# Cross-covariance attention into a gated feed-forward on one core: output weights on another queue, moved norm roots, a plain first chunk

## The chip, the cores and the metric

The kernel runs on one core of one Trainium2 chip. The core has four compute engines with instruction streams of their own: TensorE (PE, matrix products into the accumulator memory PSUM), VectorE (DVE), ScalarE (ACT) and GpSimd (POOL). A fifth, SyncE (SP), only issues transfers here. DMA transfers are issued from SP, ACT and POOL, and all move data through the same 16 DMA engines. An engine executes its instructions in program order, so an instruction that waits holds up everything behind it on that engine.

The metric is device time in microseconds: the median of several executions. A difference below about 0.5% is no difference.

## The reference, cut to what matters

```python
B, N, C = 4, 6016, 256                       # q, k, v: float32, times 0.1
qn = q / (norm(q, axis=1) + 1e-6)            # norms run over the 6016 rows
kn = k / (norm(k, axis=1) + 1e-6)
s  = kn^T @ qn / tau                         # 256 x 256 for each batch
a  = softmax(s)                              # over the last axis
x  = (v @ a).reshape(24064, 256)
gate = sigmoid(x @ w_gate)                   # 256 -> 1536
out  = (gate * (x @ w_val)) @ w_out          # 1536 -> 256
```

## The kernel before

A batch is handled in two parts. The first makes its attention matrix. For each of its 47 row tiles (128 rows each) `score` multiplies q against k into one PSUM tile (`ps_s`, two products of 128x256), and the squares of q and k are summed for the norms. For batch 0 this is the head of the program, and it runs at the pace at which q and k are loaded. For batches 1 to 3 it runs beside the feed-forward of the batch before. The softmax is then folded into the weights: `gh` multiplies the exponentials by `w_gate` and `w_val` and scales by the row sums (`rrow`, and half of it, `rhalf`). This gives G and H, so that v goes straight into the feed-forward.

The second part is the feed-forward. It runs over 12 chunks of a batch, four row tiles (512 rows) each and three in the last one, and in a chunk over 12 **slots**, one for each 128 of the 1536 hidden columns. So a batch has slots 0 to 143, and slot 120 is the first slot of chunk 10. In a slot `glu` does two products with G into `ps_gate`, two with H into `ps_val`, a tanh on ACT (`g_sb`), and one DVE instruction that makes a row of `hT` from `g_sb` and `ps_val`. `ps_gate` and `ps_val` have two buffers each.

The output product of a chunk runs one chunk later, seven matmuls of 128x128 in each slot (`run_work`). It doesn't multiply plainly. Two row tiles (a pair p) and two column halves are combined as in Strassen's scheme: seven products in place of eight, over sums of `hT` blocks (`a_sum`, DVE, tile `sums`, five for each half of the hidden columns) and sums of weight blocks (`sum_w_out`, POOL, tile `w_sums`). `part` copies three partial products out on ACT (`m_sb`) and adds them on POOL; `whole` copies the four results (`out_sb`) and corrects them on POOL. A chunk with four row tiles has two pairs; their order is in `ORDER`. The last chunk of a batch has three tiles: one lone pair and a single tile, whose 12 products of 128x256 (`single`) stand ahead of the pair's. The last chunk of all is finished behind the loop by `end_rows` and `last_rows`.

The order is written out by hand. Each engine's instructions stand in the order in which the Python code emits them, and `side_work` hangs extra calls on slots with `at(slot, function)`. What it hangs there for the next batch n:

- `load_qk`, `load_v` on POOL's queue; `score`, `acc_square`, `acc_add` up to slot 96; `acc_fold` at slots 97 to 117
- `norms_mm` at 119 (sums the squares over rows on PE), `root_seed` at 120 (two DVE instructions: first guess for the inverse root), `root_steps` at 120 (POOL: four Newton steps of four instructions and one product)
- `norms_inv` at 123 (two DVE instructions that read the root `r`), `spread_both` at 124 (PE: four passes that spread `r` over the partitions), `copy_rk` at 125, `scale_x` at 126 and 127, `exps` at 128 and 129, `sums_both` at 131, `gh` from 132 on

For batch 0, `load_w_out` at slots 0, 1 and 2 loads the output weights (three pieces of 512 KB, float32). The call stands at a slot, but it is on SP, which has nothing else to do, so only the piece's buffer holds it back. `copy_w_out` casts a piece on POOL and `sum_w_out` makes the sums of weights, 15 instructions. All other weights and nearly all q, k and v come over POOL's queue, which casts from float32 to bfloat16 on the way; its order is q and k of batch 0, v chunk 0, six weight pieces, v chunk 1.

In the head, `busy(n)` issues n products on constants that only keep PE busy.

Of the kernel before, what the change touches and what calls it, by code (L numbers as in the profile page):

```python
# [53 lines left out]
def kernel(  # L54
# [138 lines left out]
    def load_w_out(n):  # L193
        w_f32[n] = f32pool.tile([P, TPC, C], FP32, tag="f32", name="w_f32")
        nc.sync.dma_start(
            out=w_f32[n], in_=moe_w_out.rearrange("(t p) c -> p t c", p=P)[:, n * TPC : (n + 1) * TPC, :]
        )
# [156 lines left out]
    def root_steps(b):  # L354

        s = st[b]
        x, y = s["sq_n"], s["y"]
        t = attp.tile([P, 2 * CB], FP32, tag="tn", name="t_n")
        s["r"] = attp.tile([P, 2 * CB], FP32, tag="r", name="r")
        for _ in range(4):  # L360
            nc.gpsimd.tensor_tensor(out=t, in0=x, in1=y, op=ALU.mult)  # L361
# [3 lines left out]
        nc.gpsimd.tensor_tensor(out=s["r"], in0=x, in1=y, op=ALU.mult)  # L365
# [51 lines left out]
    def sums_both(b):  # L417
# [13 lines left out]
        invert(r, ps_r, 1e-9, 1.0)  # L431
        half = attp.tile([P, CB], FP32, tag="rhalf", name="rhalf", bufs=2)
        nc.vector.tensor_scalar(out=half, in0=r, scalar1=0.5, scalar2=None, op0=ALU.mult)
        s["rrow"] = [[x[:, i : i + 1] for i in range(CB)] for x in (r, half)]
# [119 lines left out]
    def out_work(b, ci):  # L554
# [5 lines left out]
        states = [{} for _ in range(half)]  # L560

# [49 lines left out]
        def single(s, f):  # L611
            if f == 0:
                states[0]["single"] = pso.tile([P, CH], FP32, tag="o", name="ps_o")
            ps = states[0]["single"]
# [63 lines left out]
    adds, ends = [], []  # L678
    for g, (t0, nt) in enumerate(groups0):
# [17 lines left out]
        if g == last0:  # L697
            norm_mms(ps_n0, acc, TPC, True, False)
            for n, (end, rows_n) in enumerate(ends):
                norm_mms(ps_n0, end, rows_n, False, n == len(ends) - 1, (1, 0) if n else (0, 1))  # L700
        for u in range(nt):
            score(0, t0, u)
        if n_acc - 4 <= g < n_acc:
            busy(1)
    st[0]["n"] = ps_n0
    norms_sqrt(0)
    nc.scalar.preload_act_table(ACT.Exp)
    norms_inv(0)
    copy_s(0, 0)
    copy_s(0, 1)  # L710
    busy(3)
# [14 lines left out]
    gh_store(0, 0, ps_first, False)  # L726
    gh(0, 1, psg, "g", act=True)
# [3 lines left out]
    def side_work(b):  # L731
# [7 lines left out]
        for ci in range(NCH):  # L739
# [34 lines left out]
        for i in range(6):  # L774
            at(8 * FC + 1 + 4 * i, acc_fold, n, *divmod(i, 3))
# [6 lines left out]
        at(s0 + 7, copy_rk, n)  # L782
        at(s0 + 8, scale_x, n, 0)
        at(s0 + 9, scale_x, n, 1)
        at(s0 + 10, exps, n, 0)
        at(s0 + 11, exps, n, 1)
        at(s0 + 13, sums_both, n)
        at(s0 + 13, gh_tiles, n)
        for i in range(len(gh_order)):
            at(s0 + 14 + i, gh, n, i, *((pss, "s"), (psm, "m"))[i % 2])  # L790
# [7 lines left out]
    for b in range(B):  # L798
        side = side_work(b)
        for ci in range(NCH):  # L800
            final = (b, ci) == (B - 1, NCH - 1)
            for f in range(FC):
                first = (b, ci, f) == (0, 0, 0)
                glu(b, ci, f, (lambda: gh(0, 4, pso, "o", act=False)) if first else None)
                if prev is not None:
                    if f == 4:
                        store()
                    if f in NEXT_SLOTS:
                        a_sum(*prev, 1, NEXT_SLOTS[f])
                    run_work(work, 1 / max(1, FC - 2 * final - f))  # L810
                if f in OWN_SLOTS and not final:
# [48 lines left out]
```

## Time and profile before

| | |
|---|---|
| median of 9 executions | 828.92 us (827.39 to 836.74) |
| the profiled execution | 831.71 us, of which its span is 829.9 us |
| granted TensorE clock, mean | 0.984 |
| PE / DVE / ACT / POOL busy | 96% / 87% / 63% / 43% |
| DMA moved | 78.24 MB, mean 94 GB/s |
| chain that ended last | PE 89%, DMA 4%, POOL 3%, DVE 2% |

The span runs from the first instruction to the last; 1.8 us of the execution lie around it. Rows of the timeline give start, duration, engine, line, operation, tile written and tile read, shapes and count, and in brackets the idle time of the engine before the row and what ended it. Every product has line L127, since one helper issues them all, so tiles are what tells them apart. A matmul's duration includes its way through the array; products that follow each other start closer together than that, so the distance between starts is the cost. Rows of the view by windows give the stretch, its length, the busy time of PE, weight loads (PEld), DVE, ACT and POOL with their counts, the granted clock, the share of the DMA engines and GB/s. Bytes are counted as written, so a load that casts from float32 counts half of what it reads.

### The profile page before, as it was taken

To read this page: it belongs to the slowest core of one execution; us is meant where nothing else is said; L and a number is where in the kernel's file an instruction comes from. 1 tells how busy PE (TensorE), PEld (TensorE's weight loads), DVE (VectorE), ACT (ScalarE), POOL (GpSimd) and SP (SyncE) were. 2 spreads that over 40 slices of the span, in tenths; PEclk is the share of its full clock that TensorE was granted. 3 is DMA by queue.
4 is the path that set the end of the run, shared out by engine and by line. 5 is a ranking of instruction groups with operands and counts; after the bars stand their busy time and mean duration, and the time that the engine had idled before them with its cause. 6 is when DMAs were issued, how large, how long until landed. Compare 5 with 4: busy or idle time off the path is not lost.

```text
span 829.9 us, 17993 instructions
## 1 busy us (share of the span) xinstructions
PE 793.2 (96%) x6790; PEld 503.9 (61%) x6790; DVE 725.3 (87%) x1240; ACT 526.8 (63%) x887; POOL 358.7 (43%) x583
## 2 busy tenths in 40 slices
PE   3699999999899999999899999999989999999997
PEld 2446666666566666666566666666656566666665
DVE  4788999999688999999887999999978899898994
ACT  3557777765466777775566777776656565666663
POOL 3455445434443444434543454433353234434442
PEclk9799999999899999999999999999999999999999
DMA  9984767532557756422446566623422332433301
GB/s 228 218 156 89 118 101 133 102 64 46 86 117 112 114 102 133 92 52 67 92 82 112 96 127 109 116 52 88 60 52 52 84 64 52 90 64 78 70 27 71
DMA packets 77929, 78.24 MB, mean 94 GB/s; under 512 B 50705, under 2 KB 55825, under 8 KB 77841
## 3 DMA queue, kind: packets, MB, share of 16 engines
q0 software_dynamic: 21216, 38.02, 28.3%
q1 hardware_dynamic: 56336, 38.48, 20.6%
q8 instruction: 53, 0.87, 0.4%
q10 hardware_dynamic: 288, 0.59, 0.2%
q14 instruction: 36, 0.29, 0.1%
HBM read 78.64 MB, written 24.64 MB: 124 GB/s over the span
## 4 chain that ended last, share of the span: by engine, by line
PE 89%; DMA 4%; POOL 3%; DVE 2%; issue 1%; ACT 1%; POOLq 0%
PE ps_gate L127 28%; PE ps_val L127 28%; PE ps_o L127 26%; PE ps_s L127 4%; DMA k_sb<-in_k_dram 4%; PE ps_gh L127 2%; DVE hT L517 1%; ACT g_sb L516 1%; PE ps_rk L127 0%; POOL t_n L363 0%; POOL t_n L362 0%; DVE sums L539 0%; POOL t_n L361 0%; POOL y_n L364 0%; POOL out_sb L607 0%
## 5 line engine op out<-in xcount | busy, mean ns | idle before, releaser
L516 ACT ACTIVATE g_sb<-ps_gate 128x512 f32<-128x512 f32 (+1 forms) x576 | 338.3, 588 | 244.0 <-PE ps_gate L127 232.5
L517 DVE SCALAR_TENSOR_TENSOR hT<-g_sb,ps_val 128x512 bf16<-128x512 f32 (+1 forms) x576 | 384.1, 670 | 72.4 <-ACT g_sb L516 57.2
L127 PE MATMUL ps_val<-vT,gh_H 128*128 128x512 bf16 (+1 forms) x1152 | 339.4, 376 | 0.9 <-DVE hT L517 0.8
L127 PE MATMUL ps_gate<-vT,gh_G 128*128 128x512 bf16 (+1 forms) x1152 | 339.5, 376 | 0.0
L539 DVE TENSOR_TENSOR sums<-hT 128x768 bf16<-128x768 bf16 (+1 forms) x470 | 288.3, 613 | 0.0
L127 PEld LDWEIGHTS <-sums 128*128 128x128 bf16 x2730 | 188.5, 98 | 89.9 <-issue 4.4
L127 PEld LDWEIGHTS <-gh_H 128*128 128x128 bf16 x1152 | 113.1, 98 | 133.7 <-issue 4.3
L606 POOL TENSOR_TENSOR out_sb<-out_sb,m_sb 128x256 f32<-128x256 f32 x91 | 78.4, 862 | 236.3 <-ACT out_sb L598 224.1
L127 PE MATMUL ps_o<-w_sums,sums 128*128 128x128 bf16 x1638 | 158.9, 219 | 1.7 <-DVE sums L539 1.7
L592 POOL TENSOR_TENSOR m_sb<-m_sb 128x128 f32<-128x128 f32 x91 | 42.7, 469 | 183.0 <-ACT m_sb L591 183.0
L127 PEld LDWEIGHTS <-hT 128*128 128x128 bf16 x1176 | 85.3, 98 | 44.5
L127 PEld LDWEIGHTS <-gh_G 128*128 128x128 bf16 x1152 | 97.3, 98 | 15.2 <-DVE gh_G L466 0.4
L127 PE MATMUL ps_o<-w_out_sb,sums 128*128 128x128 bf16 x1092 | 99.6, 221 | 2.0 <-ACT m_sb L591 1.9
L127 PE MATMUL ps_o<-w_sums,hT 128*128 128x128 bf16 x1092 | 97.7, 219 | 0.0
L127 PE MATMUL ps_s<-k_sb,q_sb 128*128 128x256 bf16 x376 | 71.9, 295 | 19.1 <-DMA k_sb<-in_k_dram 12.1
L607 POOL TENSOR_TENSOR out_sb<-out_sb 128x256 f32<-128x256 f32 x91 | 80.0, 879 | 7.1
L598 ACT COPY out_sb<-ps_o 128x512 f32<-128x512 f32 x91 | 53.4, 586 | 14.0 <-PE ps_o L127 11.2
L278 DVE TENSOR_TENSOR acc<-acc,sq 128x1024 bf16<-128x1024 bf16 (+1 forms) x66 | 60.4, 915 | 0.0
L593 POOL TENSOR_TENSOR m_sb<-m_sb 128x128 f32<-128x128 f32 x91 | 55.4, 608 | 7.1
L240 ACT ACTIVATE sq<-k_sb 128x1024 bf16<-128x1024 bf16 (+2 forms) x44 | 44.8, 1028 | 16.7 <-DMA k_sb<-in_k_dram 16.7
L127 PEld LDWEIGHTS <-q_sb 128*128 128x128 bf16 x376 | 33.7, 105 | 25.0 <-issue 12.6
L591 ACT COPY m_sb<-ps_o 128x384 f32<-128x384 f32 x91 | 43.6, 479 | 4.3 <-PE ps_o L127 2.0
(81 smaller groups left out, 309.1 us busy)
## 6 DMA issues: line engine op xcount, KB each, us to landing
out_dram<-out_sb SPq DMA_DIRECT2D x44, 512.0 KB, 3.4
v_sb<-in_v_dram POOLq DMA_DIRECT2D x44, 256.0 KB, 5.2
q_sb<-in_q_dram POOLq DMA_DIRECT2D x35, 256.0 KB, 4.3
k_sb<-in_k_dram POOLq DMA_DIRECT2D x35, 256.0 KB, 5.2
q_sb<-in_q_dram POOLq DMA_DIRECT2D x4, 512.0 KB, 14.0
k_sb<-in_k_dram POOLq DMA_DIRECT2D x4, 512.0 KB, 16.3
w_f<-in_moe_w_out_dram SPq DMA_DIRECT2D x3, 512.0 KB, 18.4
out_dram<-out_sb SPq DMA_DIRECT2D x3, 384.0 KB, 2.8
```

Of the source, the lines that this page charges most:

```text
L127: nc.tensor.matmul(out, lhsT=lhsT, rhs=rhs, start=start, stop=stop, **kw)
L240: nc.scalar.activation(out=sq[:, :nt, :], in_=src[:, :nt, :], func=ACT.Square)
L278: nc.vector.tensor_tensor(out=acc[:, :nt, :], in0=acc[:, :nt, :], in1=st[b]["sq", w][:, :nt, :], op=ALU.add)
L516: nc.scalar.activation(out=g_sb[:, :n], in_=ps_gate[:, :n], func=ACT.Tanh, scale=0.5)
L517: nc.vector.scalar_tensor_tensor(out=hts[b, ci][:, f, :n], in0=g_sb[:, :n], scalar=1.0, in1=ps_val[:, :n], op0=ALU.add, op1=ALU.mult,)
L539: nc.vector.tensor_tensor(out=sums[b, ci, g][:, m, :, : half * P], in0=hT[:, f0 + k0 : f1 : 2, ds(r0 * half * P, half * P)], in1=hT[:, f0 ...
L591: nc.scalar.copy(m, states[p]["ps"][:, : 3 * P].rearrange("p (n c) -> p n c", c=P))
L592: nc.gpsimd.tensor_tensor(out=m[:, 1, :], in0=m[:, 1, :], in1=m[:, 2, :], op=ALU.add)
L593: nc.gpsimd.tensor_tensor(out=m[:, 2, :], in0=m[:, 1, :], in1=m[:, 0, :], op=ALU.add)
L598: nc.scalar.copy(o[:, p : p + half + 1 : half, :], states[p]["ps"].rearrange("p (t c) -> p t c", c=C),)
L606: nc.gpsimd.tensor_tensor(out=ends, in0=ends, in1=states[p]["m"][:, 1:3, :], op=ALU.add)
L607: nc.gpsimd.tensor_tensor(out=ends, in0=ends, in1=mids, op=ALU.subtract)
```

## The change

Seven edits:

1. The three `w_out` loads are issued on POOL's queue, behind the other weights and v chunk 1, in place of SP. Their casts are at slot 8 and the sums of weights at slots 10 to 18.
2. For the next batch: three Newton steps in place of four; `norms_mm` at slot 117, `root_seed` and `root_steps` at 118, `norms_inv` at 124, `spread_both` at 125, `copy_rk` at 126, both `scale_x` at 127; the rest stays on its slots. `acc_fold` is closer together (97 to 115).
3. The single tile of a three-tile chunk stands between the lone pair's `z1` and `x2`, no longer ahead of the pair.
4. In the last chunk of all, the work is shared over all 12 slots (before: 10), and each `a_sum` of the second half stands one slot earlier.
5. Chunk 0 of batch 0 makes its output plainly: 48 products of 128x256, no `a_sum`, no `part`, no `whole`.
6. In the head: the last scores stand ahead of the last norm products; scores are copied out of PSUM ahead of the root, one half on ACT; q's norm is multiplied in by two DVE instructions (`scale_q`), and k's by one instruction for each block; `rhalf` is made after the first store of G.
7. `busy` gets other counts and places: 4, 1, 4, 4, 2 behind groups 6 to 10 (before: 1 each behind 7 to 10), then 2 (before 3).

```diff
-    def load_w_out(n):
+    for n in range(FC // TPC):
         w_f32[n] = f32pool.tile([P, TPC, C], FP32, tag="f32", name="w_f32")
-        nc.sync.dma_start(
+        nc.gpsimd.dma_start(
...
-        for _ in range(4):
+        for _ in range(3):
...
-        nc.vector.tensor_copy(out=s["x"][:, j, :], in_=s["s"][:, j, :])
+        (nc.scalar.copy if j else nc.vector.tensor_copy)(out=s["x"][:, j, :], in_=s["s"][:, j, :])
+
+    def scale_q(b, j):
+        s = st[b]
+        x = s["x"][:, j, :]
+        nc.vector.tensor_scalar(out=x, in0=x, scalar1=s["r"][:, j : j + 1], scalar2=None, op0=ALU.mult)
...
-        for j in range(CB):
-            nc.vector.scalar_tensor_tensor(
-                out=y[:, j, :],
-                in0=s["x"][:, j, ds(i * P, P)],
-                scalar=s["r"][:, j : j + 1],
-                in1=s["rk"][i],
-                op0=ALU.mult,
-                op1=ALU.mult,
-            )
+        nc.vector.tensor_tensor(
+            out=y,
+            in0=s["x"][:, :, ds(i * P, P)],
+            in1=s["rk"][i].rearrange("p (o c) -> p o c", o=1).to_broadcast([P, CB, P]),
+            op=ALU.mult,
+        )
...
+        plain = (b, ci) == (0, 0)
...
-        if nt % 2:
-            for f in range(FC):
-                work.append((2, single, nt - 1, f))
+        if plain:
+            return [(2, single, t, f) for t in range(nt) for f in range(FC)]
         for p, name in ORDER:
             if p < half:
                 for i in range(FC // 2):
                     work.append((1, product, p, name, i))
+                if nt % 2 and name == "z1":
+                    for f in range(FC):
+                        work.append((2, single, nt - 1, f))
...
-        if n_acc - 4 <= g < n_acc:
-            busy(1)
+        busy(fill.get(g, 0))
...
-                    at(i, load_w_out, i)
-                    at(i + 2, copy_w_out, i)
+                    at(8, copy_w_out, i)
                 for n, m in enumerate((1, 0, 3, 2, 4)):
                     for i in range(FC // TPC):
-                        at(3 + 3 * n + i, sum_w_out, m, i)
+                        at(10 + 2 * n, sum_w_out, m, i)
...
-        s0 = 10 * FC - 2
-        at(s0 + 1, norms_mm, n)
-        at(s0 + 2, root_seed, n)
-        at(s0 + 2, root_steps, n)
-        at(s0 + 5, norms_inv, n)
-        at(s0 + 6, spread_both, n)
+        s0 = 10 * FC - 3
+        at(s0, norms_mm, n)
+        at(s0 + 1, root_seed, n)
+        at(s0 + 1, root_steps, n)
+        at(s0 + 7, norms_inv, n)
+        at(s0 + 8, spread_both, n)
...
-                    if f in NEXT_SLOTS:
-                        a_sum(*prev, 1, NEXT_SLOTS[f])
-                    run_work(work, 1 / max(1, FC - 2 * final - f))
-                if f in OWN_SLOTS and not final:
+                    if f + final in NEXT_SLOTS and prev != (0, 0):
+                        a_sum(*prev, 1, NEXT_SLOTS[f + final])
+                    run_work(work, 1 / (FC - f))
+                if f in OWN_SLOTS and not final and (b, ci) != (0, 0):
```

How this stands on the engines, at two places. The first is POOL at the start of the program, behind the weights. `v_sb` is a chunk of v, `w_f32` a piece of the output weights, `q_sb` and `k_sb` are the first rows of batch 1. Before:

```order
L184 DMA w_val2_175<-in_moe_w_val_dram 128x2x512
L147 DMA v_sb_183<-in_v_dram 128x1024
L147 DMA v_sb_476<-in_v_dram 128x1024
L200 CAST w_out_sb_176<-w_f32_478 128x1024
L137 DMA q_sb_511<-in_q_dram 128x1024
L137 DMA k_sb_513<-in_k_dram 128x1024
L200 CAST w_out_sb_176<-w_f32_493 128x1024
```

Now:

```order
L184 DMA w_val2_175<-in_moe_w_val_dram 128x2x512
L147 DMA v_sb_183<-in_v_dram 128x1024
L195 DMA w_f32_186<-in_moe_w_out_dram 128x4x256
L195 DMA w_f32_188<-in_moe_w_out_dram 128x4x256
L195 DMA w_f32_190<-in_moe_w_out_dram 128x4x256
L147 DMA v_sb_501<-in_v_dram 128x1024
L137 DMA q_sb_529<-in_q_dram 128x1024
L137 DMA k_sb_531<-in_k_dram 128x1024
L200 CAST w_out_sb_176<-w_f32_186 128x1024
```

The three loads have come over from SP; they stand ahead of v chunk 2 and of batch 1's first rows, and the casts stand behind these.

The second place is POOL at the turn from batch 0 to batch 1, slots 116 to 120. The `out_sb` rows are the two corrections of `whole` (one pair each), `t_n` begins the Newton steps, and the DMAs are the loads of slot 120. Before:

```order
L606 TENSOR_TENSOR out_sb_2848<-out_sb_2848,m_sb_2752 128x2x128
L607 TENSOR_TENSOR out_sb_2848<-out_sb_2848 128x2x128
L606 TENSOR_TENSOR out_sb_2848<-out_sb_2848,m_sb_2789 128x2x128
L607 TENSOR_TENSOR out_sb_2848<-out_sb_2848 128x2x128
L147 DMA v_sb_2941<-in_v_dram 128x1024
L137 DMA q_sb_2943<-in_q_dram 128x1024
L137 DMA k_sb_2945<-in_k_dram 128x1024
L361 TENSOR_TENSOR t_n_2951<-sq_n_2947,y_n_2948 128x4
```

Now, the last rows of the Newton steps and what stands behind them; the first pair's two `out_sb` rows are directly ahead of the steps:

```order
L363 TENSOR_SCALAR t_n_2869<-t_n_2869 128x4
L364 TENSOR_TENSOR y_n_2866<-y_n_2866,t_n_2869 128x4
L365 TENSOR_TENSOR r_2870<-sq_n_2865,y_n_2866 128x4
L615 TENSOR_TENSOR out_sb_2814<-out_sb_2814,m_sb_2753 128x2x128
L616 TENSOR_TENSOR out_sb_2814<-out_sb_2814 128x2x128
L147 DMA v_sb_2923<-in_v_dram 128x1024
L137 DMA q_sb_2925<-in_q_dram 128x1024
L137 DMA k_sb_2927<-in_k_dram 128x1024
```

The root is made ahead of the second pair's correction and of the three loads, no longer behind them.

More of the change, by code (lines that the diff above doesn't have):

```diff
@@ L431, in sums_both, with half_rows @@
         invert(r, ps_r, 1e-9, 1.0)
+        s["rsum"] = r
+        s["rrow"] = [[r[:, i : i + 1] for i in range(CB)]]
+    def half_rows(b):
+        s = st[b]
         half = attp.tile([P, CB], FP32, tag="rhalf", name="rhalf", bufs=2)
-        nc.vector.tensor_scalar(out=half, in0=r, scalar1=0.5, scalar2=None, op0=ALU.mult)
-        s["rrow"] = [[x[:, i : i + 1] for i in range(CB)] for x in (r, half)]
+        nc.vector.tensor_scalar(out=half, in0=s["rsum"], scalar1=0.5, scalar2=None, op0=ALU.mult)
+        s["rrow"].append([half[:, i : i + 1] for i in range(CB)])
     def gh_tiles(b):
@@ L612, in single @@
             if f == 0:
-                states[0]["single"] = pso.tile([P, CH], FP32, tag="o", name="ps_o")
-            ps = states[0]["single"]
+                singles[s] = pso.tile([P, CH], FP32, tag="o", name="ps_o")
+            ps = singles[s]
             mm(ps[:, :C], hT[:, f, ds(s * P, P)], w_out_sb[:, f, :], f == 0, f == FC - 1)
@@ L617, in single @@
                 nc.scalar.copy(out_tile(b, ci)[:, s, :], ps[:, :C])
-        if nt % 2:
-            for f in range(FC):
-                work.append((2, single, nt - 1, f))
+                if plain and s == nt - 1:
+                    stores.append((b, ci))
+        if plain:
+            return [(2, single, t, f) for t in range(nt) for f in range(FC)]
         for p, name in ORDER:
@@ L678 @@
     adds, ends = [], []
+    fill = {6: 4, 7: 1, 8: 4, 9: 4, 10: 2}
     for g, (t0, nt) in enumerate(groups0):
@@ L708 @@
     norms_inv(0)
-    copy_s(0, 0)
-    copy_s(0, 1)
-    busy(3)
+    scale_q(0, 0)
+    scale_q(0, 1)
+    busy(2)
     spread_k(0, 0, pso, "o")
@@ L726 @@
     gh_store(0, 0, ps_first, False)
+    half_rows(0)
     gh(0, 1, psg, "g", act=True)
```

27 lines of the change are left out of this document (16 added, 11 removed).

## The prediction

> **What bounds the kernel now.** I read the page first, then the waits, then windows around each place where PE stops.
>
> ```profile
> PE 793.2 (96%) x6790; PEld 503.9 (61%) x6790; DVE 725.3 (87%) x1240; ACT 526.8 (63%) x887; POOL 358.7 (43%) x583
> ```
>
> PE is busy for all but 36.7 us of a span of 829.9 us. So a gain has to come from those 36.7 us, from slots in which PE runs at a lower clock, or from fewer products; the change has hardly any of the last. The view of waits (us in total, times, longest) says what PE stops for:
>
> ```profile
> PE ps_s L127 <- DMA k_sb<-in_k_dram: 12.1, 5, 3.4
> PE ps_rk L127 <- DVE r L370: 9.3, 3, 3.4
> DVE r L369 <- POOL r L365: 7.8, 3, 2.9
> PE ps_o L127 <- ACT m_sb L591: 1.9, 3, 0.6
> ```
>
> The first row is the head, which waits for loads. The next two are one chain, three times, once at each turn to a new batch: POOL's root, DVE's inverse, PE's spread. The fourth is the lone pair. Each has an edit.
>
> **Head: the output weights go behind the rest.** The first two rows are windows; DMA is saturated in both (share above 1).
>
> ```profile
> 6.00:33.00 27.00, 14.95 (x73) 9.95 (x74) 16.26 (x26) 10.87 (x11) 5.74 (x11) 0.75 1.07 230
> 38.00:48.00 10.00, 9.64 (x60) 4.82 (x60) 7.79 (x20) 6.90 (x12) 8.94 (x13) 1.00 1.22 207
> ```
> ```profile
> 1.19 6.11 SPq L195 DMA_DIRECT2D w_f<-in_moe_w_out_dram  x3
> ```
> ```profile
> DMA to landing us min/median/max: 13.1/18.4/26.1
> ```
>
> The three pieces (1.57 MB) are issued from 1.19 us to about 7 and land at 14 to 33 us, in the middle of q and k, on which PE waits. From 6 to 33 us 27 x 230 GB/s = 6.2 MB arrive. Without the 1.57 MB, 4.6 MB remain, all cast loads, and cast loads alone get 207 GB/s in the second window: 22.4 us in place of 27. Some of w_out's bytes arrived before 6 us, which I leave out. **Term: -4.4 us.** Bounds: 0 (something other than loads sets the pace) and -6.8 (1.57 MB at 230 GB/s). The `busy` products, ten more of at most 0.63 us, lie in PE's 12 idle us of the first window; without that cover the last six would cost up to 3.8 us.
>
> ```profile
> 31.29 0.63 PE L127 MATMUL ps_busy<-ones_wide,ones_bf 128*128 128x512 bf16 x1
> ```
>
> The shorter root chain in the head (edit 6) I cost at nothing, between +0.4 and -0.4:
>
> ```profile
> 34.57 0.71 POOL L184 DMA_DIRECT2D w_val<-in_moe_w_val_dram  x1 [0.43 <-DMA q_sb<-in_q_dram]
> ...
> 41.79 1.02 PE L127 MATMUL ps_gh<-w_val,e_sb 128*128 128x512 bf16 x4
> ```
> ```profile
> w_val<-in_moe_w_val_dram POOLq DMA_DIRECT2D x1, 256.0 KB, 7.2
> ```
>
> The first piece of `w_val` lands at 34.57 + 7.2 = 41.8 us, where its products start. Whatever is saved ahead of it waits for this load, which moves with the term above.
>
> Does w_out come too late now? v chunk 1, ahead of it:
>
> ```profile
> 38.60 1.12 POOL L147 DMA_DIRECT2D v_sb<-in_v_dram  x2
> ...
> 58.96 0.55 PE L127 MATMUL ps_o<-w_sums,hT 128*128 128x128 bf16 x7
> ```
> ```profile
> v_sb<-in_v_dram POOLq DMA_DIRECT2D x2, 256.0 KB, 9.9
> ```
>
> It lands at about 48.5, now 44. Then 1.57 MB take between 3.8 us (twice 207 GB/s, since these loads aren't halved by a cast) and 6.8 us: 48 to 51. The last cast adds about 1 us. The first output product stood at 58.96, now about 54.5: 2.5 to 5 us are left. The loads behind it (v chunk 2, q and k of batch 1) are for slot 14 and later; the sums of weights are needed from slot 24.
>
> **Chunk 0 made plainly.** Three products of 128x256 take 0.32 us, seven of 128x128 take 0.39 (distance to the next row):
>
> ```profile
> 249.31 0.49 PE L127 MATMUL ps_o<-w_out_sb,hT 128*128 128x256 bf16 x3
> 249.63 0.59 PE L127 MATMUL ps_gate<-vT,gh_G 128*128 128x512 bf16 x2
> ```
> ```profile
> 243.61 0.55 PE L127 MATMUL ps_o<-w_sums,sums 128*128 128x128 bf16 x7
> 244.00 0.59 PE L127 MATMUL ps_gh<-w_val,e_sb 128*128 128x512 bf16 x2
> ```
> ```profile
> 57.47 0.59 PE L127 MATMUL ps_val<-vT,gh_H 128*128 128x512 bf16 x2 [0.53 <-DVE hT L517]
> ```
>
> 48 x 0.107 = 5.1 us against 12 x 0.39 = 4.7: +0.5 on PE. Ten `a_sum` leave DVE, and PE's wait of 0.53 us for DVE goes. **Term: 0**, from -1 to +1.
>
> **The three turns.** A window of four plain slots, then the four slots of each turn, slots 124 to 127:
>
> ```profile
> 204.60:209.61 5.01, 5.01 (x50) 3.12 (x47) 4.39 (x10) 2.97 (x5) 4.01 (x9) 1.00 0.36 100
> 209.61:221.65 12.04, 8.66 (x52) 5.27 (x50) 5.50 (x11) 3.62 (x7) 4.91 (x18) 0.72 0.59 90
> 410.18:420.92 10.74, 7.36 (x52) 4.63 (x50) 5.20 (x11) 3.62 (x7) 5.08 (x18) 0.84 0.67 101
> 609.45:619.16 9.71, 7.16 (x51) 4.43 (x49) 5.19 (x11) 3.62 (x7) 4.50 (x15) 0.82 0.32 59
> ```
>
> Four slots take 5.01; `ps_rk` adds 0.6 at full clock (0.68 busy in the head). Lost are 6.4, 5.1 and 4.1 us, **15.6 in all**: 9.3 as PE's wait, the rest because the granted clock stays low behind it (0.72, 0.84, 0.82). The first turn in full:
>
> ```profile
> 202.13 0.93 POOL L607 TENSOR_TENSOR out_sb<-out_sb 128x256 f32<-128x256 f32 x1
> ...
> 207.10 0.17 DVE L345 TENSOR_SCALAR y_n<-sq_n 128x4 int32<-128x4 int32 x1
> ...
> 208.57 0.23 POOL L361 TENSOR_TENSOR t_n<-sq_n,y_n 128x4 f32<-128x4 f32 x1
> ...
> 210.23 0.55 DVE L539 TENSOR_TENSOR sums<-hT 128x768 bf16<-128x768 bf16 x1
> ...
> 213.42 0.20 POOL L365 TENSOR_TENSOR r<-sq_n,y_n 128x4 f32<-128x4 f32 x1
> ...
> 213.65 0.40 DVE L369 TENSOR_SCALAR r<-r 128x4 f32<-128x4 f32 x1 [2.88 <-POOL r L365]
> 214.08 0.18 DVE L370 RECIPROCAL r<-r 128x4 f32<-128x4 f32 x1
> ...
> 214.41 1.20 PE L127 MATMUL ps_rk<-ident_f,r 128*128 128x128 f32 x4 [3.38 <-DVE r L370]
> ```
>
> 17 POOL instructions take 208.57 to 213.62, 0.30 us each. Now 13, 3.9 us. They start when the seed is there, two slots (2.5 us) earlier: 204.8, and POOL is free from 203.06. So `r` is there at 208.7, and DVE asks for it a slot later than before, at about 212.0: 3.3 us to spare. The second pair's correction and the loads of slot 120 shift by some 3.4 us behind the steps. That is covered: the v loaded there is transposed at slot 134, and SP only stores at slot 124.
>
> What is late next is DVE. Without POOL's wait it would have begun the inverse at 210.78 and finished at 211.36; with the 0.15 us seen between inverse and spread, PE could go on at 211.5, and it stood ready at 214.41 - 3.38 = 211.03. The new order has the same work ahead of the inverse (one `hT`, one `sums`), so about 0.5 us stays; I take 0.6 for each turn. Bounds: 0, and 2.0 if all extra DVE work of slots 124 to 131 (0.6 inverse, two `scale_x`, row sums) shows. **Term: -(15.6 - 1.8) = -13.8.** This holds if 0.6 us doesn't lower the clock. The smallest that did was the third turn's 2.55; a wait of 0.6 at the lone pair (about 255) didn't:
>
> ```profile
> 613.42 1.19 PE L127 MATMUL ps_rk<-ident_f,r 128*128 128x128 f32 x4 [2.55 <-DVE r L370]
> ```
> ```profile
> 250.00:260.00 10.00, 9.38 (x76) 5.72 (x74) 7.60 (x15) 6.53 (x11) 2.16 (x4) 1.00 0.97 128
> ```
>
> The Trainium skill, "TensorE: Matmul & The Clock Gate", Part 1, has PE's clock fall to half after an idle window of about 3.4 us. The third turn's window with 0.82 followed a wait of only 2.55, so there the trace doesn't agree, and the measurement decides; by the page that turn's slow slots would not have come from its wait, 1.5 us of the sum would stay, and the time would be about 812.
>
> **Lone pair.** Three waits for `m_sb`, 1.9 us. With the single's 12 products (1.3 us) between `z1` and `x2` the copy is hidden. But `z1` now comes up to four slots earlier, nearer to the `a_sum` of slot 1 that it reads:
>
> ```profile
> L539 DVE TENSOR_TENSOR sums<-hT 128x384 bf16<-128x384 bf16 x30 | 10.7, 357 | 0.0
> ```
>
> At worst one such sum shows each time (0.36). **Term: -1.5**, from -0.8 to -1.9.
>
> **Last chunk.**
>
> ```profile
> 807.25:822.38 15.13, 13.34 (x135) 9.35 (x133) 9.25 (x19) 7.80 (x17) 5.50 (x9) 1.00 0.09 36
> ```
> ```profile
> 821.28 0.59 ACT L598 COPY out_sb<-ps_o 128x512 f32<-128x512 f32 x1 [0.28 <-PE ps_o L127]
> ...
> 822.75 0.73 POOL L607 TENSOR_TENSOR out_sb<-out_sb 128x256 f32<-128x256 f32 x1
> ...
> 825.00 1.51 PE L127 MATMUL ps_end<-w_out_sb,hT 128*128 128x128 bf16 x24
> ```
>
> PE idles 1.79 us, since 8.4 products in a slot overtake the sums. Seven in a slot, with sums one slot earlier, shouldn't. The last pair's copy and correction now run behind the last slot (0.59 and two of about 0.73, some 2.3 us with their gaps), beside the 4.1 us of the last rows' products (822.38 to 826.5). **Term: -1.6**, from -1.0 to -1.8.
>
> **Sum.** -4.4 + 0 - 13.8 - 1.5 - 1.6 = -21.3 on 831.71: 810.4. This execution lies 2.8 us above the median of 828.92; from the median the same sum gives 807.6. The turns of one program lose 6.4, 5.1 and 4.1 us, so this kind of loss differs between executions and goes in any case; I stay near its own sum: **810**.
>
> **Rivals.**
> - *The last is DVE, not POOL.* DVE is 87% busy. If the inverse comes late enough at each turn that the clock falls again, each loses at least the third turn's 4.1 us: 15.6 - 12.3 = 3.3 gained in place of 13.8, 821. For it: 0.5 us of lateness is already in the rows. Against: 2.55 is the smallest pause that lowered the clock. 0.12.
> - *w_out comes late.* PE waits at slot 12 of batch 0. Landing 5 us later than reckoned costs some 2 us of waiting and as much in clock: 814 to 816. 0.07. The Trainium skill, "SBUF — State Buffer", section "SBUF: two separate sides", speaks for it: descriptors of loads issued from GpSimd are not written while certain VectorE instructions hold the port that both share. The weights issued on POOL at 33 to 39 us, with DVE at work, landed 6.6 to 9.0 us later, so the trace doesn't show it.
> - *The head doesn't do what it says.* Buffers or casts set the pace of q and k, not bytes: 814.8. Against: DMA share 1.07 throughout. 0.06.
> - *Slower than before.* PE has its longest stretches at full clock between turns, some 190 us. Without the pauses the granted clock could fall from slot 125 of batch 0 on, for about 600 us. At 0.95 that costs 32 us: 842. It decides from 0.965, where 21.3 us are used up. Against: inside those stretches the clock is 1.00 to the end. 0.03.
>
> **How the numbers follow.** The forecast has 0.72, with 806 to 814 from its bounds. The range 805 to 819 takes in the late weights and the unshortened head, and leaves out about half of the first rival's and all of the slower case. Faster by over 0.5% means below 824.8 (0.5% is about what a measurement here can tell from no change): all but the slower case and a small remainder, 0.95; the same 0.02; slower 0.03.
>
> **What would show it.** Right: the last k of batch 0 lands near 33 us and slot 0 starts near 38 (before 42.72); no row in which DVE's `r` waits for POOL; four slots of a turn in 6.2 us at clock 1.00; no PE wait for `m_sb`; none over 0.2 us in the last chunk. Wrong: PE waits for `w_out_sb` at slot 12, a turn's window at a clock below 0.95, or a head as long as before.

## The result, and the profile after

The changed kernel takes **812.96 us** (median of 10 executions, 812.55 to 813.92); the kernel before, run beside it, 830.38 us (32 executions, 827.19 to 840.58). The ratio is 0.979, with a 95% interval from 0.978 to 0.981. The prediction was 810, with a range of 805 to 819. Besides being faster, the changed kernel repeats better: its executions lie within 1.4 us of each other, those of the kernel before within 13.

The profiled execution takes 812.78 us, its span is 810.9 us (before 829.9). Its page, and the rows of its view of waits that answer to those of before (us in total, times, longest):

```profile
PE 787.9 (97%) x6764; PEld 501.1 (62%) x6764; DVE 719.8 (89%) x1229; ACT 526.0 (65%) x888; POOL 352.0 (43%) x566
```
```profile
PE ps_s L127 <- DMA k_sb<-in_k_dram: 7.1, 4, 2.1
...
PE ps_val L127 <- DVE hT L524: 2.0, 4, 0.6
...
PE ps_rk L127 <- DVE r L370: 1.9, 4, 0.8
```

The wait for loads fell from 12.1 to 7.1 us, the wait for `r` from 9.3 to 1.9 (0.8 of it in the head), those of DVE for POOL's root and of PE for `m_sb` are gone. The middle row has grown. In the kernel before it was:

```profile
PE ps_val L127 <- DVE hT L517: 0.8, 2, 0.5
```

Of these two waits the longer, 0.53 us in chunk 0, went with the plain chunk, as the prediction has it; the other, 0.30, is still there. Three new ones of 0.58 us came, which the prediction did not have.

To see where the time went, I set the start of each slot (its tanh) in the two traces side by side, and took how much the difference grew in each stretch:

| stretch | predicted | measured |
|---|---|---|
| start to slot 0 | -4.4 | -3.6 |
| chunks 0 to 2 of batch 0 | 0 | -0.25 |
| chunk 8 of batches 0 to 2 (the folds) | not priced | **+2.2** |
| the three turns | -13.8 | -14.3 (6.0, 4.7, 3.6) |
| lone pairs | -1.5 | -2.0 (0.7, 0.5, 0.7) |
| last chunk to the end | -1.6 | -1.2 |
| sum | -21.3 | -19.1, and the spans differ by 19.0 |

The four slots of each turn, by windows of the changed kernel:

```profile
207.08:213.19 6.11, 5.73 (x49) 3.65 (x48) 5.21 (x12) 3.08 (x6) 4.16 (x8) 1.00 0.78 150
401.72:407.76 6.04, 5.73 (x49) 3.65 (x48) 5.19 (x12) 3.08 (x6) 4.14 (x8) 1.00 0.81 150
596.52:602.70 6.18, 5.72 (x49) 3.65 (x48) 5.50 (x12) 3.08 (x6) 3.00 (x6) 1.00 0.56 131
```

They take 6.1 us where they took 12.0, 10.7 and 9.7, at a clock of 1.00. The window of chunk 8, for which the prediction has no term, in the kernel before and in the changed one:

```profile
174.96:190.00 15.04, 15.04 (x134) 9.35 (x133) 15.01 (x27) 9.13 (x17) 6.03 (x9) 1.00 0.39 71
```
```profile
171.08:186.87 15.79, 15.21 (x134) 9.38 (x133) 15.76 (x28) 9.15 (x18) 6.01 (x9) 1.00 0.31 68
```

In both DVE is busy all the time (15.01 of 15.04, 15.76 of 15.79). PE was too, before; now it idles 0.58 of 15.79. So DVE's work became longer there, and PE waited for it. The timeline of that place in the changed kernel:

```profile
182.38 0.73 POOL L615 TENSOR_TENSOR out_sb<-out_sb,m_sb 128x256 f32<-128x256 f32 x1 [2.80 <-ACT out_sb L607]
182.52 1.00 DVE L546 TENSOR_TENSOR sums<-hT 128x768 bf16<-128x768 bf16 x1
...
183.18 0.92 POOL L616 TENSOR_TENSOR out_sb<-out_sb 128x256 f32<-128x256 f32 x1
...
183.44 0.81 DVE L295 CAST fold<-two 128x256 bf16<-128x256 f32 x1
...
185.37 0.59 PE L127 MATMUL ps_val<-vT,gh_H 128*128 128x512 bf16 x2 [0.58 <-DVE hT L524]
```

The CAST of the third fold step now stands at slot 104, beside POOL's correction of the first pair, and takes 0.81 us; other CASTs of this form take 0.28. It ends just behind POOL's second instruction (184.25 and 184.10).

Two executions among the runs below, of 1389 and 2934 us, were plainly disturbed and are left out of the medians.

### The profile page after: what moved, and what is told of

It is laid out like the page before. It is cut to its first block, busy times and chain, and to the rows that moved or that the text cites. A ratio compares the mean times of both kernels' runs of the same rounds, so it can differ in the third digit from the quotient of the medians.

```text
span 810.9 us, 17905 instructions
## 1 busy us (share of the span) xinstructions
PE 787.9 (97%) x6764; PEld 501.1 (62%) x6764; DVE 719.8 (89%) x1229; ACT 526.0 (65%) x888; POOL 352.0 (43%) x566
## 4 chain that ended last, share of the span: by engine, by line
PE 90%; DVE 5%; DMA 2%; issue 1%; ACT 1%; POOL 1%; DVEq 0%; POOLq 0%
PE ps_gate L127 28%; PE ps_val L127 28%; PE ps_o L127 26%; PE ps_s L127 4%; PE ps_gh L127 2%; DVE hT L524 2%; DMA k_sb<-in_k_dram 2%; DVE sums L546 1%; ACT g_sb L523 1%; PE ps_busy L127 0%; POOL q_sb L137 0%; DVE fold L295 0%; PE ps_rk L127 0%; DVE two L292 0%; DVE acc L278 0%
## 5 line engine op out<-in xcount | busy, mean ns | idle before, releaser
L546 DVE TENSOR_TENSOR sums<-hT 128x768 bf16<-128x768 bf16 (+1 forms) x460 | 280.3, 609 | 0.0
L127 PEld LDWEIGHTS <-sums 128*128 128x128 bf16 x2670 | 183.1, 98 | 82.4 <-DVE sums L546 0.3
L127 PE MATMUL ps_o<-w_sums,sums 128*128 128x128 bf16 x1602 | 154.8, 219 | 0.1
L127 PEld LDWEIGHTS <-hT 128*128 128x128 bf16 x1200 | 88.3, 98 | 46.7
L601 POOL TENSOR_TENSOR m_sb<-m_sb 128x128 f32<-128x128 f32 x89 | 41.9, 470 | 156.6 <-ACT m_sb L600 156.4
L127 PE MATMUL ps_o<-w_out_sb,sums 128*128 128x128 bf16 x1068 | 96.2, 219 | 0.0
L127 PE MATMUL ps_o<-w_sums,hT 128*128 128x128 bf16 x1068 | 95.7, 219 | 0.0
L616 POOL TENSOR_TENSOR out_sb<-out_sb 128x256 f32<-128x256 f32 x89 | 77.7, 873 | 7.0
L607 ACT COPY out_sb<-ps_o 128x512 f32<-128x512 f32 x89 | 52.2, 586 | 14.3 <-PE ps_o L127 11.6
L602 POOL TENSOR_TENSOR m_sb<-m_sb 128x128 f32<-128x128 f32 x89 | 53.3, 599 | 7.0
L240 ACT ACTIVATE sq<-k_sb 128x1024 bf16<-128x1024 bf16 (+2 forms) x44 | 44.8, 1027 | 12.1 <-DMA k_sb<-in_k_dram 12.1
```

Of the source, the lines that this page charges most:

```text
L127: nc.tensor.matmul(out, lhsT=lhsT, rhs=rhs, start=start, stop=stop, **kw)
L240: nc.scalar.activation(out=sq[:, :nt, :], in_=src[:, :nt, :], func=ACT.Square)
L546: nc.vector.tensor_tensor(out=sums[b, ci, g][:, m, :, : half * P], in0=hT[:, f0 + k0 : f1 : 2, ds(r0 * half * P, half * P)], in1=hT[:, f0 ...
L601: nc.gpsimd.tensor_tensor(out=m[:, 1, :], in0=m[:, 1, :], in1=m[:, 2, :], op=ALU.add)
L602: nc.gpsimd.tensor_tensor(out=m[:, 2, :], in0=m[:, 1, :], in1=m[:, 0, :], op=ALU.add)
L607: nc.scalar.copy(o[:, p : p + half + 1 : half, :], states[p]["ps"].rearrange("p (t c) -> p t c", c=C),)
```

## The experiments

**Is it the collision, or that the folds are closer?** Two kernels move the third step by one slot, to either side; the others stay at slots 97, 101, 108, 111 and 115:

```diff
-            at(8 * FC + 1 + (7 * i + 1) // 2, acc_fold, n, *divmod(i, 3))
+            at(8 * FC + (1, 5, 9, 12, 15, 19)[i], acc_fold, n, *divmod(i, 3))
```

> The changed kernel with one thing moved: the third fold step (the CAST and its difference) one slot later, from slot 104 to slot 105, where it stood before the change; the others stay. Theory (collision): the 2.2 us lost in chunk 8 of the three batches come from this CAST running beside POOL's correction of slot 104 (0.81 us in place of 0.28). Then the CAST takes 0.28 again, PE's 0.6 us waits for hT in chunk 8 go, and the time is 812.96 - 2.2 = 810.7 us, with the span near 808.7. Rival (density): six fold steps in 19 slots in place of 21 are too much for DVE wherever they stand; then a wait of 0.4 us or more stays in chunk 8 and the time is 812 to 813.

Measured: 810.60 us (808.93 to 811.17). The second kernel puts 7 where this one has 9:

> The changed kernel with the third fold step one slot earlier, at slot 103: three steps within seven slots, denser than in the change, but ahead of POOL's correction. Theory (collision): the CAST takes 0.28 us and most of the 2.2 us goes: 810.7 to 811.5 us. Rival (density): DVE is as late as or later than before, the waits for hT in chunk 8 stay at 0.6 us or grow: 813 to 814 us.

Measured: 810.63 us (810.04 to 812.60). The CAST's rows of the two, later and earlier:

```profile
181.42 1.00 DVE L546 TENSOR_TENSOR sums<-hT 128x768 bf16<-128x768 bf16 x1
182.09 0.92 POOL L616 TENSOR_TENSOR out_sb<-out_sb 128x256 f32<-128x256 f32 x1
...
182.35 0.67 DVE L524 SCALAR_TENSOR_TENSOR hT<-g_sb,ps_val 128x512 bf16<-128x512 f32 x1
...
183.42 0.28 DVE L295 CAST fold<-two 128x256 bf16<-128x256 f32 x1
```
```profile
182.12 0.28 DVE L295 CAST fold<-two 128x256 bf16<-128x256 f32 x1
```

Both are 2.3 us faster than the change, in both the difference comes off 0.74 us at a time in chunk 8 of the three batches, and PE's three waits of 0.58 us for `hT` are gone. Both still have six steps in 19 slots, and the earlier one packs the first three closer than the change does. So density is ruled out, and the collision with POOL is shown.

**Was it w_out that shortened the head?** Its loads go back to the start, the rest stays:

```diff
-        nc.gpsimd.dma_start(out=w_f32[n], ...)
+        nc.sync.dma_start(out=w_f32[n], ...)
```

> The changed kernel with the three loads of w_out on SP at the start of the program, as before the change; the rest of the head keeps its new order. Theory: the bytes of w_out set when the last k lands. It lands near 37.6 us in place of 33.7, slot 0 starts near 43.4 in place of 39.8, and the time is 812.96 + 3.6 = 816.6 us. Rival: the head became shorter through the busy products, its clock and the shorter chain of roots; then slot 0 stays below 41 and the time below 814.

Measured: 821.67 us (821.37 to 821.87), 8.7 more than the change, where 3.6 were expected. The last piece of k lands at 37.74 in place of 33.67, which is 4.1 us and the theory. Two more things came, which neither side expected:

```profile
42.79 3.01 POOL L200 CAST w_out_sb<-w_f 128x1024 bf16<-128x1024 f32 x3
43.13 3.13 DVE L440 TENSOR_SCALAR rhalf<-rrow 128x2 f32<-128x2 f32 x1
...
46.36 0.75 DVE L473 TENSOR_SCALAR gh_H<-ps_gh,rhalf 128x512 bf16<-128x512 f32 x1
...
47.17 0.61 PE L127 MATMUL ps_val<-vT,gh_H 128*128 128x512 bf16 x2 [2.87 <-DVE gh_H L473]
```

The three casts of w_out stand at slot 8 in the code, but POOL only waits for its data. With w_out landed early, it casts them back to back just when DVE makes `rhalf`, 256 numbers. That takes 3.13 us, and PE waits 2.87. In the changed kernel:

```profile
38.97 0.16 DVE L440 TENSOR_SCALAR rhalf<-rrow 128x2 f32<-128x2 f32 x1
```

Another 1.7 us go in the first three slots of chunk 0. They are the clock's: just behind PE's pause of 2.87 us it stands at 0.50 for 3.4 us, half of which is lost (the window shows the clock in its third column from the right):

```profile
48.06:51.46 3.40, 3.40 (x10) 1.20 (x9) 1.87 (x3) 1.24 (x2) 3.40 (x6) 0.50 1.12 211
```

So 4.1 us of landing, 2.9 of waiting and 1.7 of clock make up the 8.7. In the changed kernel the casts come at 44.94 and later, each by itself, because their data come late; the late load does more than free the loads ahead of it.

**Does the head's root chain cost something?** Undone, so that it is as before the change: the norm products of the last rows stand ahead of the last scores, both copies are on DVE behind the inverse, and the weights have their old form (the lines below are shortened).

```diff
-        for u in range(nt): score(0, t0, u)
         if g == last0:
             for n, (end, rows_n) in enumerate(ends): norm_mms(ps_n0, end, ...)
+        for u in range(nt): score(0, t0, u)
...
-    copy_s(0, 0); copy_s(0, 1)
     norms_sqrt(0); preload; norms_inv(0)
-    scale_q(0, 0); scale_q(0, 1)
+    copy_s(0, 0); copy_s(0, 1)
```

> The changed kernel with the head's root chain as before the change: norm products of the last rows ahead of the last scores, both copies of the scores on DVE behind the inverse, the weights from four combined DVE instructions. w_out stays behind, the busy products too. Theory: the last k lands 4.4 us earlier in the changed kernel, and 0.8 us of it are given back because the square root now stands behind a copy on ACT and the last scores (34.82 against the last score at 33.67; before 38.25 against 38.08). So the chain from the last score to the first ps_gate shrinks from 5.4 to 4.6 us and slot 0 starts near 39.0: 812.2 us. Rival (what the prediction said): the chain costs nothing, the length stays at 5.4 us and the time at 812.7 to 813.2.

Measured: 811.71 us, 1.2 less than the change. But the reason is not the one given. The last landing (the square of the last k waits for it), the last scores and the first `ps_gate`, in this kernel and in the change, and the landing of the kernel before:

```profile
32.47 0.29 DVE L242 TENSOR_TENSOR sq<-k_sb 128x256 bf16<-128x256 bf16 x1 [0.23 <-DMA k_sb<-in_k_dram]
...
34.08 0.38 PE L127 MATMUL ps_s<-k_sb,q_sb 128*128 128x256 bf16 x2
...
38.65 0.61 PE L127 MATMUL ps_gate<-vT,gh_G 128*128 128x512 bf16 x2
```
```profile
33.67 0.29 DVE L242 TENSOR_TENSOR sq<-k_sb 128x256 bf16<-128x256 bf16 x1 [1.53 <-DMA k_sb<-in_k_dram]
33.67 0.38 PE L127 MATMUL ps_s<-k_sb,q_sb 128*128 128x256 bf16 x2
...
39.11 0.60 PE L127 MATMUL ps_gate<-vT,gh_G 128*128 128x512 bf16 x2
```
```profile
37.62 0.29 DVE L242 TENSOR_TENSOR sq<-k_sb 128x256 bf16<-128x256 bf16 x1 [0.23 <-DMA k_sb<-in_k_dram]
```

From the last scores it is 4.57 us against 5.44, as expected, but only because the last scores stand behind the norm products. From the landing it is 6.2 against 5.4. Here k landed 1.2 us earlier, with the same order of loads. In nine profiled kernels with w_out behind, the square of the last k starts at 32.4 us in two and at 33.7 to 33.9 in seven. So this theory falls as I had put it. One pair compares like with like: the kernel with the third fold step later has the changed order and also had its k early (32.42), and its first `ps_gate` stands at 38.01, 0.6 us ahead of this one's. There the changed order is not the slower one; what it is worth in the other executions stays open.

**The turns alone.** The kernel before with edit 2 and nothing else (folds at 97, 101, 105, 108, 111 and 115, clear of the collision; the lines are shortened):

```diff
-        for _ in range(4):
+        for _ in range(3):
...
-        at(s0 + 1, norms_mm, n)      # 119; seed and steps 120, inverse 123, spread 124
+        at(s0, norms_mm, n)          # 117; seed and steps 118, inverse 124, spread 125
```

> The kernel before with the turn's edits alone: three Newton steps, the chain of a turn at the new slots, row weights read by the old two kinds of instructions moved with it, and folds at slots 97, 101, 105, 108, 111 and 115. Theory: the turns lose their wait and with it the low clock behind it; the profile shows a clock of 1.00 in slots 124 to 127 and -14.3 us against the kernel before: near 816 us. Rival (the clock falls for another reason than the pause): windows of the turns stay at 0.72 to 0.84 and only the waits of 9.3 us, less the 2 us that stay in the changed kernel, go: 823 us.

Measured: 817.93 us, 13.8 less than the kernel before beside it (831.72). Slot by slot the turns give 6.0, 4.7 and 3.6 us, as in the full change, and the first turn's window reads:

```profile
210.66:216.77 6.11, 5.73 (x49) 3.65 (x48) 5.38 (x12) 3.08 (x7) 4.04 (x8) 1.00 0.79 148
```

So the term of the turns stands by itself, and the low clock goes with the pause.

**Place or length of the chain?** Four Newton steps again in the changed kernel (`range(4)`):

> The changed kernel with four Newton steps in place of three. Theory: the root is ready 3.1 us before DVE takes it, four more POOL instructions at 0.31 us are 1.24 us, so nothing changes: 812.96, within 0.3 us; the place of the chain made the gain, not its length. Rival: the shorter chain is needed; then the turns lose 1.24 us each or more: 816 us and above.

Measured: 814.03 us, 1.1 more: neither nothing nor 1.24 for each turn. The root is in time; something else moved. The changed kernel's first turn, then this kernel's:

```profile
205.81 0.20 POOL L365 TENSOR_TENSOR r<-sq_n,y_n 128x4 f32<-128x4 f32 x1
...
206.77 0.72 POOL L616 TENSOR_TENSOR out_sb<-out_sb 128x256 f32<-128x256 f32 x1
...
208.43 0.73 DVE L546 TENSOR_TENSOR sums<-hT 128x768 bf16<-128x768 bf16 x1
...
209.09 0.16 DVE L369 TENSOR_SCALAR r<-r 128x4 f32<-128x4 f32 x1
```
```profile
208.23 0.20 POOL L365 TENSOR_TENSOR r<-sq_n,y_n 128x4 f32<-128x4 f32 x1
...
209.58 0.73 POOL L616 TENSOR_TENSOR out_sb<-out_sb 128x256 f32<-128x256 f32 x1
209.62 1.10 DVE L546 TENSOR_TENSOR sums<-hT 128x768 bf16<-128x768 bf16 x1
...
210.64 0.19 DVE L369 TENSOR_SCALAR r<-r 128x4 f32<-128x4 f32 x1
...
211.10 0.71 PE L127 MATMUL ps_rk<-ident_f,r 128*128 128x128 f32 x4 [0.68 <-DVE r L370]
```

The root is ready at 208.43 and DVE takes it 2.2 us later (with three steps at 206.01, and 3.1 us later), so the fourth step fits. But POOL's correction runs behind the steps, and now it lies on the `sums` just ahead of the inverse, which takes 1.10 in place of 0.73. PE waits 0.68 in place of 0.38. The turns grow by 0.3, 0.35 and 0.76 us. (In the profiled execution slot 0 stands 1.3 us later as well, by the clock in the head; see the next experiment.)

**How long a pause lowers the clock?** The kernel before with three steps and nothing else shortens the pauses.

> The kernel before with three Newton steps in place of four and nothing else. PE's waits for the inverse at the turns were 3.38, about 3.3 and 2.55 us; each shrinks by 1.24 us, to 2.1, 2.1 and 1.3. That alone is -3.7 us, 826 us. The run shows from which pause on the granted clock falls. Theory: it falls behind each of these pauses as before (0.72 to 0.84), so only about 3.7 us go. Rival: pauses near 2 us leave it at 1.00; then the clock's part of the 15.6 us (6.3 us) goes too: 820 us.

Measured: 825.61 us, ratio 0.994 (0.991 to 0.998). The run that gave its profile:

> The kernel before with three Newton steps once more, since the profile of the run before this is of no use. Pauses of PE at the turns of 2.1, 2.1 and 1.3 us. Theory: the granted clock falls behind each of them as before and the turns lose 3.7 us less: 826 us. Rival: it stays at 1.00 and the loss shrinks to the pauses: 820 us.

Measured: 824.02 us. PE's waits at the three turns, then the windows of their four slots:

```profile
213.35 0.68 PE L127 MATMUL ps_rk<-ident_f,r 128*128 128x128 f32 x4 [2.27 <-DVE r L370]
```
```profile
409.86 0.68 PE L127 MATMUL ps_rk<-ident_f,r 128*128 128x128 f32 x4 [2.27 <-DVE r L370]
```
```profile
607.19 0.68 PE L127 MATMUL ps_rk<-ident_f,r 128*128 128x128 f32 x4 [1.44 <-DVE r L370]
```
```profile
210.29:218.26 7.97, 5.70 (x49) 3.65 (x48) 5.05 (x12) 3.05 (x6) 3.76 (x11) 1.00 0.80 125
406.80:416.44 9.64, 7.37 (x49) 4.50 (x48) 5.50 (x13) 3.14 (x7) 3.87 (x11) 0.82 0.66 103
604.97:612.11 7.14, 5.70 (x49) 3.65 (x48) 5.30 (x12) 3.05 (x7) 3.07 (x9) 1.00 0.51 67
```

The same pause of 2.27 us left the clock at 1.00 at one turn and cost 1.7 us at 0.82 at the next. So neither expectation holds at all turns, though the time is near the theory's 826: at this length the clock falls or not for a reason other than the pause's length, and 2.27 us can be enough.

The price behind a pause doesn't follow its length either. In shorter windows the clock is either 1.00 or 0.50, but for the moment of a change. In the kernel before, it stood at 0.50 for 6.8 us at the first turn and for 3.4 us at the second, at the same pause of 3.38 us:

```profile
213.65:220.45 6.80, 6.04 (x27) 3.81 (x28) 3.38 (x7) 1.95 (x4) 1.93 (x4) 0.50 0.47 69
415.03:418.43 3.40, 3.40 (x16) 2.23 (x17) 1.35 (x3) 1.00 (x3) 0.09 (x1) 0.50 0.57 81
```

It was 3.4 us again at the third turn, at the second turn of this run, and with w_out first. So in these traces the price comes in steps of about 1.7 us, less what of the slow stretch lies in the pause itself. Nor is one long pause needed: in two profiled kernels with the changed kernel's head (four steps, and chunk 0 not plain, below) the clock stood at 0.50 for 3.4 and 6.8 us from about 35 us on, with no wait of PE over 1.0 and 1.2 us in the 4 us ahead. Their slot 0 stands at 41.10 and 42.30, where the change has 39.81. The Trainium skill, "TensorE: Matmul & The Clock Gate", Part 1, has activity judged in windows of about 3.4 us that run freely. That one pause can go either way, and that the slow stretches have one or two times this length, agrees with free windows. That a pause well below one window is enough does not agree with an idle window being needed; the measurement decides.

**The lone pair.** The single tile's products ahead of the pair's again:

```diff
+        if nt % 2:
+            for f in range(FC): work.append((2, single, nt - 1, f))
         for p, name in ORDER:
...
-                if nt % 2 and name == "z1":
-                    for f in range(FC): work.append((2, single, nt - 1, f))
```

> The changed kernel with the 12 products of the single tile ahead of the lone pair's again. Theory: the three waits of PE for m_sb (0.6 us each) come back and with them the three slots that were shortened by 0.73, 0.50 and 0.73 us: +2.0, 814.9 us. Rival: the gain in these chunks came from elsewhere (the shorter turn just ahead of them): 813.

Measured: 814.47 us, 1.5 more. The wait is back, as it stood in the kernel before, and the three places grow by 0.73, 0.50 and 0.73 us, with no difference elsewhere in the slots (the end behind the slots, which varies, is 0.7 us shorter in this execution):

```profile
PE ps_o L127 <- ACT m_sb L600: 1.9, 3, 0.6
```

**The last chunk.** The old sharing in the changed kernel:

```diff
-                    if f + final in NEXT_SLOTS and prev != (0, 0):
-                        a_sum(*prev, 1, NEXT_SLOTS[f + final])
-                    run_work(work, 1 / (FC - f))
+                    if f in NEXT_SLOTS and prev != (0, 0):
+                        a_sum(*prev, 1, NEXT_SLOTS[f])
+                    run_work(work, 1 / max(1, FC - 2 * final - f))
```

> The changed kernel with the last chunk's products shared out as before, 8.4 in a slot and none in the last, and its sums one slot later. Theory: PE gets its 1.8 us of waits in the last chunk back and the last pair's store leaves one slot earlier, ahead of the end's stores: the stretch from slot 0 of the last chunk to the end is longer by 1.2 us, 814.1 us, and the last write lands about 3.0 us behind its issue, not 4.5. Rival: the tail is set by the last stores, so the share changes nothing: 813.

Measured: 814.33 us, 1.4 more. PE's waits are back, and from slot 0 of the last chunk to the end it takes 22.15 us (change 20.79, before 21.97). In the four profiled kernels with the old sharing this stretch is 21.96 to 22.15 us, in the nine with the new one 19.28 to 21.18, so the sharing shows clear of the spread:

```profile
PE ps_o L127 <- DVE sums L546: 1.7, 2, 1.0
```

**Chunk 0 not plain**, with all sums of weights at slot 8 (`plain = False`, and `at(8, sum_w_out, m, i)`):

> The changed kernel with chunk 0 of the first batch made like the others, by the seven products with sums, and the sums of weights all made at slot 8. Theory: PE saves 0.4 us of products, the weights' sums (15 of 0.7 us from 49 us on) come just in time, and DVE has ten a_sum more beside POOL's work, which slows each: +0.3 to +1.5, 813.3 to 814.5 us. Rival: the plain chunk costs PE more than it saves, 812.5 us; or PE waits for w_sums at slot 12 and further, 816 us.

Measured: 811.98 us (811.60 to 813.93), below the expected range, and nearest to the rival by which the plain chunk costs PE more than it saves; the head's spread covers the difference. From slot 0 to slot 0 of the last chunk, which leaves the head and the tail out, it takes 750.52 us against 750.30: 0.2 us for the plain chunk. In chunks 0 and 1 alone it is 0.5; the rest comes back in one slot of batch 2, where the run with the old root chain has the same -0.2. PE waits nowhere for `w_sums`. So the plain chunk is not what lets w_out come late. (Slot 0 stood 2.5 us later here than in the change, at a low clock. The first output product, at 58.01, would otherwise stand near 55.5, and by an estimate from the 15 sums, which end at 61.41, the first three are there at 51.4.)

**A version with the repairs**: the third fold at slot 105, the norm products ahead of the last scores and the square root ahead of the copies, no `busy` ahead of the last group, and the last two pairs stored separately (of the diff, only this last is shown):

```diff
+            if (b, ci) == (B - 1, NCH - 2):
+                nc.sync.dma_start(out=out_rows[b][:, t0 + p : t0 + p + half + 1 : half, :], ...)
+            elif p == half - 1:
```

> The changed kernel with four things mended: the third fold step at slot 105; in the head the norm products of the last rows ahead of the last scores and the square root ahead of the two copies; no busy products ahead of the last group; and the last two pairs stored each on its own, so that only 256 KB are left to write behind the last chunk. By my theories: folds -2.2, head -0.6 to -1.2, tail up to -1.2 of the 1.5 us given back there: 812.96 - 4.0 to -4.6 = 808.4 to 809.0 us. If the folds alone count: 810.7.

Measured: **809.86 us** (809.49 to 810.43), ratio 0.975 (0.972 to 0.978); it lies below every execution of both kernels. The folds give their 2.2 us. The head gives nothing (slot 0 at 39.94, change 39.81), so the mended chain isn't worth what I had thought. The tail takes 19.92 us, within the spread of the nine. The fold alone had 810.60, so nothing else is shown to help.

## Why the prediction was right, step by step

- **The three turns.** Right in mechanism and size: -14.3 for -13.8. The root is ready 3.1 us before DVE takes it (reckoned 3.3), DVE becomes the last by a few tenths, and such waits leave the clock at 1.00. Edit 2 alone gives the same. The third turn, where 1.5 us might have stayed behind a pause of only 2.55, runs at 1.00 like the others. The side step that the moved correction is "covered" held, but not for its reasons alone: they were v and the store, and with four steps the correction lands on DVE's `sums`, of which the prediction did not think.
- **Head.** Right in mechanism, mis-sized by 0.8. The last landing moved by 3.95 us, not 4.4 (the working itself, 27 less 22.4, gives 4.6), and the chain from there (the square of the last k) to slot 0 grew from 5.82 to 6.14 us, where it was costed at nothing, within 0.4. The size differs between executions: of nine, two landed 1.2 us earlier still, and two had a low clock behind the landing.
- **w_out in time.** Right. PE has no wait for it; POOL's first cast begins at 44.94, the last ends at 48.86 (reckoned last landing 48 to 51, and 1 us), the first output product stands at 54.53. The slack is 5.7 us, where 2.5 to 5 were reckoned (the figures give 5.5 for the upper end).

```profile
44.94 1.04 POOL L200 CAST w_out_sb<-w_f 128x1024 bf16<-128x1024 f32 x1 [3.05 <-DMA w_f<-in_moe_w_out_dram]
...
47.82 1.04 POOL L200 CAST w_out_sb<-w_f 128x1024 bf16<-128x1024 f32 x1 [0.33 <-DMA w_f<-in_moe_w_out_dram]
```

- **Chunk 0**: right, -0.25 over the first three chunks, and 0.2 to 0.5 by the experiment.
- **Lone pair**: right in mechanism, -2.0 for -1.5. No `a_sum` showed behind the earlier `z1`, so the bound of -1.9 was the value.
- **Last chunk**: mis-sized by 0.4, and only because two larger errors nearly cancel. The slots got 2.6 us shorter (14.45 to 11.81 from slot 0 to the first end product), 1.0 more than reckoned, but the last write ends 1.5 us later behind its issue: 4.49 us here, 3.03 before. The last pair's store of 512 KB is now issued 2.4 us into the end's products (before 1.1), just ahead of the last stores:

```profile
804.34 0.33 SPq L654 DMA_DIRECT2D out_dram<-out_sb  x1
...
805.73 1.10 SPq L676 DMA_DIRECT2D out_dram<-end  x1
...
806.41 0.35 ACTq L676 DMA_DIRECT2D out_dram<-end  x1
```

  In four profiled kernels with the old sharing this last distance is 3.02 to 3.21 us, in eight with the new one and the whole store 2.98 to 4.88. That the stores contend fits these numbers but is not shown: the kernel with the split store has 3.34, inside the spread of the whole one.
- **What the prediction left out**: "`acc_fold` is closer together" was in the change, and no step of the sum priced it. That is the +2.2 us, the largest error of the sum, and the -21.3 would have been -19.1 with it. That this is the measured sum to a tenth is luck: the errors of the other terms (+0.8, -0.25, -0.5, -0.5 and +0.4) cancel. The rule that every moved instruction counts was kept for POOL's steps and not for DVE's folds, though DVE is the engine that has no slack in chunk 8.

The rivals fell: DVE did not take POOL's place at the turns (0.4 us of PE's wait at the first), w_out was not late, the head did shorten, and the clock is 0.998 over the span without the pauses.

## What to carry to other kernels

A moved instruction has to be priced by what runs beside it on other engines, not only by its queue: three of the surprises here were a DVE instruction that came to lie beside POOL's work and took two, three and twenty times as long. Where an engine is busy 15.01 of 15.04 us, moving one of its instructions by one slot can be a term of the sum: it cost 0.74 us each time on the one slot, and nothing on its neighbours. A pause of PE can cost 1.5 to 3.0 us in clock behind it, on top of 2.3 to 3.4 us of waiting, or nothing, and the same pause is not priced alike at two turns. So such a pause is worth removing, and a sum that holds one is uncertain by about that much.

## What the runs showed of the hardware that was not expected

DVE instructions of some forms take longer beside POOL's work on SBUF. The CAST took 0.81 us in place of 0.28, `sums` 1.00 to 1.10 in place of 0.55, and `rhalf`, 256 numbers, 3.13 in place of 0.16, beside three POOL casts in a row (3.01 us together). The instruction `hT`, which reads PSUM and SBUF, keeps its 0.67 to 0.69, beside POOL (233 rows of the changed kernel's timeline) or not (254). The Trainium skill, "SBUF — State Buffer", section "SBUF: two separate sides", has one port pair that POOL and some DVE instructions take as a whole, each for its whole instruction; CAST, `sums` and `hT` agree with it. Here `rhalf` did not get its turn between the casts: it ended 0.46 us behind the last of the three. What held it so long is not shown.

In windows of 0.5 us the granted clock of PE is 1.00 or 0.50, but for those in which it changes. Its slow stretches behind the pauses of 2.27 to 3.38 us last 3.4 or 6.8 us, and the longer pause does not always have the longer stretch.
